# A 212-for-235 transfer rate in a planner, ten wide idle products for nineteen narrow ones, and new due-time offsets, in a Fourier filter followed by a gated convolution

## The chip, the cores and the metric

The kernel runs on one core of one Trainium2 chip. The metric is the device time of one execution in microseconds; the time before is the median of three runs. Lower is better.

## The reference

The input `x` has 8 batches of 3200 positions with 256 channels, in float32. Each batch is transformed along the positions, mixed across channels as complex numbers, soft-thresholded at 0.01 and transformed back; the result goes through a causal five-tap convolution that makes a gate, a product with `w_val` that the gate multiplies, and a product with `w_out`.

```python
X = np.fft.rfft(x, axis=1);  Xr, Xi = X.real, X.imag
Yr = Xr @ w_r - Xi @ w_i + b_r
Yi = Xr @ w_i + Xi @ w_r + b_i
Yr, Yi = (np.sign(v) * np.maximum(np.abs(v) - 0.01, 0) for v in (Yr, Yi))
y = np.fft.irfft(Yr + 1j * Yi, n=3200, axis=1)
gate = sigmoid(sum(conv_w[k] * shifted(y, k) for k in range(5)))
out = (gate * (y @ w_val)) @ w_out
```

## The kernel before, in words

**The transform is split as 3200 = 50 x 64.** Every batch goes through these stages; the names are those of the profile.

1. `p` (L583; L549 for the first batch): the 50-point part. `x` tiles of 50 rows come in by L577 (L540), each tile as two transfers of 200 KB that use ten of the sixteen DMA engines. Four products of 64 output rows with 512 columns fill one PSUM tile; ScalarE copies it out and it goes to a DRAM buffer `a_dram` (L597, L561).
2. `s` (L634): `a` is read back from DRAM (L615) with the other index on the partitions, and a full-float32 product with the constants `f_sb` gives the spectrum with channels on the partitions. There are 13 steps `u` a batch, all but the last with two frequency groups each, so two halves of two products.
3. ScalarE and VectorE split the spectrum into a rounded high part and the rest (`xs`), and make the sum of real and imaginary parts (`sx`) (L684 to L696).
4. The complex mixing by three real products: `k_bank` (L709, six products of 128 x 256) and `y_ps` (L704, twelve). The last step of a batch has a special form (L667, L668). VectorE adds `k_bank` and the bias (L715), then `y_ps` (L718); ScalarE and VectorE threshold (L722, L724) into `tp`.
5. `z_ps` (L747, sixteen products of 64 x 64 weights for two steps; L739 for the last step alone): the inverse 64-point part. ScalarE copies it out (L758, L755), and it goes to `z_dram` (L765).
6. `y_p` (L803): the inverse 50-point part for a block of 400 positions, read back from `z_dram` by L788 (again 200 KB on ten engines). ScalarE copies it into `y_sb` (L810).
7. For each of 8 blocks a batch: VectorE's taps `acc` (L860, four for each half of the channels), ScalarE's first tap and sigmoid (L857, L871), the split of `y` (L360, L362), `v_ps` (L835, twelve products), VectorE's multiplication by the gate (L902), the split into `gated`, `o_ps` (L835), the copy to `o` (L926) and the store to `out` (L928). The last blocks of the last batches use unsplit float32 weights `w_late` (L831).

**TensorE works in three manners.** Products on pieces of 64 x 64 of the array (`p`, `z_ps`, `y_p`), which the code marks "q"; full-float32 products (`s`, L469, L739 and the `w_late` products); and rounded products of 128 x 128 (`k_bank`, `y_ps`, `v_ps`, `o_ps`), marked "r".

**A planner in the program sets the order.** `Plan.add` takes pieces with an engine, a duration, tiles read and written, and a due time `at`. `Plan.order` walks forward in its own model of time: on each engine it considers the pieces that can begin within a small slack of the earliest, and takes the one with the smallest due time; on TensorE it adds or subtracts offsets (`stay`, `crowd`, `hold`, `together`) that make it stay with or away from "q" products. The due times are step numbers plus offsets from the table `O`; one step is a thirteenth of a batch. `PIPE` tells the planner what all transfers of so many engines together move in bytes per ns. None of these numbers is in an instruction: they only set the order in which instructions stand on each engine's queue (TensorE, VectorE, ScalarE, and SyncE for nearly all DMAs), and each queue is then worked off in order.

**PSUM and buffers.** `ps_2` has two tiles of two banks that `p`, `z_ps`, `y_p`, `v_ps` and `o_ps` take in turn, so each of these groups waits until the one two places earlier has been read out. `y_ps` has one tile, `k_bank` two halves. `a` has two tiles of four frequency groups.

**Idle products.** In the first batch TensorE has nothing to do while `x` comes in and `a_dram` makes its way to DRAM and back. `warm` (L947 to L951) issues float32 products on zeros into a PSUM tile that nobody reads: 4 first, one after each `p`, and `WARM[2]` after the eighth `p` (L960, L961). L469 turns `f_sb` blocks into the inverse constants with an identity matrix; its constants come by L456.

## Time and profile before

| | |
|---|---|
| median of three runs | 883.22 us (881.55 to 883.49) |
| the profiled execution | 881.59 us, of which its span is 879.8 us |
| mean granted TensorE clock | 0.994 of full speed |
| VectorE, ScalarE busy | 759.1 us (86%), 604.9 us (69%) |
| DMA | 163.34 MB, 186 GB/s over the span |

The span runs from the first to the last instruction. A timeline row has the start and the length in us, the engine, the line, the operation, output and input, the shapes, and the number of instructions; in brackets stands how long the engine was idle before it and what ended that. One float32 product is two instructions there, so four products `p` are x8 and two steps' `z_ps` x32. Rows of one engine overlap by the pipeline; what a group takes is the distance from its start to the next group's start. In a table of stretches the columns are the stretch, its length, each engine's busy time, the granted clock, the DMA share and GB/s.

### The profile page before, as it was taken

How to read it: one execution, taken by the hardware profiler on the slowest of the kernel's cores; microseconds unless marked ns; L12 is line 12 of the kernel's file. 1: busy time of each engine (PE TensorE's matmuls, PEld its weight loads, DVE VectorE, ACT ScalarE, POOL GpSimd, SP SyncE). 2: the span in 40 equal slices, each digit the busy share in tenths (PEclk: the TensorE clock that was granted, in tenths of full speed). 3: DMA queues.
4: the chain of work that ended last, by engine and by line, in shares of the span. 5: the costliest groups of instructions: out<-in, count | busy, mean ns of one | idle time of the engine just before them, and what ended most of it. 6: DMA issues, size and time to landing. Idle time of an engine off the chain costs nothing.

```text
span 879.8 us, 24544 instructions
## 1 busy us (share of the span) xinstructions
PE 857.8 (97%) x10400; PEld 745.5 (85%) x10400; DVE 759.1 (86%) x1143; ACT 604.9 (69%) x928; POOL 3.8 (0%) x11
## 2 busy tenths in 40 slices
PE   7999999999999999999999999999999999998997
PEld 3778788878999898898899889898899999998775
DVE  2346888999989996999879997899969999899796
ACT  2456666977677766877667776877658775875664
POOL 0000000000000000000000000000100000000000
PEclk9999999999999999999999999999999999999999
DMA  6878886786554476565855576646746353423522
GB/s 212 253 244 253 240 269 197 265 251 199 165 184 146 148 218 212 177 185 172 272 168 171 175 237 205 218 122 208 244 133 202 104 171 94 142 103 110 186 76 94
DMA packets 105289, 163.34 MB, mean 186 GB/s; under 512 B 9690, under 2 KB 78172, under 8 KB 105180
## 3 DMA queue, kind: packets, MB, share of 16 engines
q1 hardware_dynamic: 103764, 158.43, 58.1%
q10 hardware_dynamic: 1416, 3.34, 1.2%
q8 instruction: 82, 1.34, 0.6%
q14 instruction: 27, 0.22, 0.1%
HBM read 82.05 MB, written 79.69 MB: 184 GB/s over the span
## 4 chain that ended last, share of the span: by engine, by line
PE 78%; DVE 15%; DMA 3%; ACT 2%; issue 1%; SPq 0%; ACTq 0%; DVEq 0%
PE y_ps L704 14%; PE o_ps L835 12%; PE v_ps L835 11%; PE s L634 9%; PE z_ps L747 8%; PE k_bank L709 7%; PE y_p L803 6%; DVE acc L860 6%; PE p L583 5%; DMA x<-in_x 2%; PE warm L951 1%; DVE acc L902 1%; PE v_ps L831 1%; DMA f_sb<-in_f 1%; DVE gated L362 1%
## 5 line engine op out<-in xcount | busy, mean ns | idle before, releaser
L860 DVE SCALAR_TENSOR_TENSOR acc<-y_sb,cw_sb,acc 128x800 f32<-128x800 f32 (+1 forms) x264 | 258.7, 1017 | 11.4 <-ACT acc L857 11.2
L704 PE MATMUL y_ps<-w_sb,xs 128*128 128x256 f32 x1152 | 157.7, 286 | 0.7 <-DVE yb L718 0.7
L835 PE MATMUL o_ps<-gated,wo_sb 128*128 128x400 f32 x756 | 153.5, 352 | 0.0
L704 PEld LDWEIGHTS y_ps<-w_sb,xs 128*128 128x128 f32 x1152 | 144.3, 190 | 8.6 <-issue 3.9
L835 PEld LDWEIGHTS o_ps<-gated,wo_sb 128*128 128x128 f32 x756 | 135.6, 189 | 3.4 <-issue 1.0
L835 PE MATMUL v_ps<-y_hl,wv_sb 128*128 128x400 f32 x660 | 130.6, 346 | 1.1 <-ACT y_sb L810 1.1
L634 PEld LDWEIGHTS s<-f_sb,a 128*128 128x128 f32 x800 | 100.3, 191 | 24.9 <-issue 19.0
L835 PEld LDWEIGHTS v_ps<-y_hl,wv_sb 128*128 128x128 f32 x660 | 118.7, 188 | 2.1 <-ACT y_sb L810 1.3
L634 PE MATMUL s<-f_sb,a 128*128 128x128 f32 x800 | 111.9, 280 | 1.3 <-DVE xs L692 1.2
L747 PE MATMUL z_ps<-tp,g_sb 64*64 64x256 f32 x1536 | 93.7, 380 | 0.0
L688 ACT CAST xs<-s 128x512 fp32r<-128x512 f32 x96 | 56.2, 586 | 43.0 <-PE y_ps L704 28.1
L709 PE MATMUL k_bank<-w_sb,xs 128*128 128x256 f32 x576 | 85.3, 283 | 0.4 <-DVE yb L715 0.4
L722 ACT ACTIVATE tp<-yb,nlam 128x512 f32<-128x512 f32 (+1 forms) x104 | 73.6, 708 | 16.5 <-DVE yb L718 9.0
L718 DVE TENSOR_TENSOR yb<-y_ps,yb 128x512 f32<-128x512 f32 x96 | 65.4, 681 | 19.9 <-PE y_ps L704 19.7
L747 PEld LDWEIGHTS z_ps<-tp,g_sb 64*64 64x64 f32 x1536 | 57.1, 133 | 27.1 <-issue 5.8
L360 ACT CAST gated<-acc 128x800 fp32r<-128x800 f32 x63 | 54.2, 861 | 37.1 <-DVE acc L902 33.5
L709 PEld LDWEIGHTS k_bank<-w_sb,xs 128*128 128x128 f32 x576 | 74.8, 188 | 5.1 <-issue 1.1
L926 ACT COPY o<-o_ps 128x800 f32<-128x800 f32 x63 | 51.9, 823 | 38.0 <-PE o_ps L835 37.8
L803 PEld LDWEIGHTS y_p<-g_sb,zl 50*64 50x64 f32 x4096 | 66.1, 135 | 13.9 <-issue 5.1
L902 DVE TENSOR_TENSOR acc<-v_ps,acc 128x800 f32<-128x800 f32 x64 | 62.9, 983 | 16.9 <-PE v_ps L835 14.1
L724 DVE SCALAR_TENSOR_TENSOR tp<-yb,tp 128x512 f32<-128x512 f32 (+1 forms) x104 | 68.8, 661 | 7.7 <-ACT tp L722 7.4
L803 PE MATMUL y_p<-g_sb,zl 50*64 50x50 f32 x4096 | 71.8, 220 | 3.4 <-issue 2.2
(80 smaller groups left out, 1028.4 us busy)
## 6 DMA issues: line engine op xcount, KB each, us to landing
zl<-z_dram SPq DMA_DIRECT2D x128, 200.0 KB
out<-o SPq DMA_DIRECT2D x63, 400.0 KB
a_dram<-s SPq DMA_DIRECT2D x120, 208.0 KB
a<-a_dram SPq DMA_DIRECT2D x96, 256.0 KB
z_dram<-z_t SPq DMA_DIRECT2D x48, 512.0 KB
x<-in_x SPq DMA_DIRECT2D x120, 200.0 KB
a_dram<-s ACTq DMA_DIRECT2D x8, 208.0 KB
x<-in_x ACTq DMA_DIRECT2D x8, 200.0 KB
```

The source lines that it names most:

```text
L634: nc.tensor.matmul(spec()[:, c, :, i, :], tl[ka][:, i0 + i, c * P:(c + 1) * P], f2_of(i), start=True, stop=True)
L688: nc.scalar.copy(out=tl[kx][:, 0:512], in_=tl[k2].rearrange("p a b -> p (a b)"))
L704: nc.tensor.matmul(p[:, 1 - r, :], xm(hx, c, r), w_sb[:, m, hw, c, :], start=k == 0, stop=k == 5)
L709: nc.tensor.matmul(p, sm(hx, c), w_sb[:, 0, hw, c, :], start=k == 0, stop=k == 5)
L718: add(at + 0.2, "DVE", dve(2 * D), lambda: nc.vector.tensor_tensor(out=yb(), in0=tl[ky], in1=yb(), op=ALU.add), [ky + (0,)], [kb + (0,)])
L722: nc.scalar.activation(out=buffer(kt, "tp", [P, 2, D])[:, 0:n], in_=tl[kb][:, 0:n], func=AF.Relu, bias=nlam)
L724: add(at + 0.2, "DVE", dve(n * D), lambda: nc.vector.scalar_tensor_tensor(out=tl[kt][:, 0:n], in0=tl[kb][:, 0:n], scalar=LAM, in1=tl[kt][: ...
L747: nc.tensor.matmul(p[e * HP:(e + 1) * HP, i, j * D:(j + 1) * D], g[i * HP:(i + 1) * HP, r, e * HP:(e + 1) * HP], tl[kts[j]][i * HP:(i + 1) ...
L803: nc.tensor.matmul(pv[h][e * HP:(e + 1) * HP, c, m, :], zt[half(h), m, c * P + e * HP:c * P + (e + 1) * HP], g2_sb[half(h), :], start=True ...
L835: nc.tensor.matmul(p[:, e, 0:TB], w[:, hw, c, e * P:(e + 1) * P], src(hy, c), start=n == 0, stop=n == 5)
L860: nc.vector.scalar_tensor_tensor(out=acc(c), in0=y_of(c, j), scalar=cw_sb[:, c, j:j + 1], in1=acc(c), op0=ALU.mult, op1=ALU.add)
L902: add(at + own("gate", b), "DVE", dve(2 * TB), lambda: nc.vector.tensor_tensor(out=gate(), in0=hn(tl[kv][:, :, 0:TB]), in1=gate(), op=ALU. ...
```

## The change

Three numbers of the planner and the idle products change; no stage, tile or buffer does. The planner is told that transfers on ten engines (`x` and `zl`) move 212 instead of 235 bytes per ns together. Nineteen idle products of 256 columns after the eighth `p` become ten of 512 columns, planned at 860 ns each. Of the offsets in `O`, 33 of 35 have new values (two lines shown). The transfers themselves are as before.

```diff
-PIPE = {10: 235, 13: 300, 16: 324}
+PIPE = {10: 212, 13: 300, 16: 324}
...
-O = {'stay': -42.085,
-     'crowd': -50.453,
+O = {'stay': -8.386,
+     'crowd': 0.988,
...
-WARM = 4, 1, 19
+WARM = 4, 1, 10
...
-    def warm(n):
+    def warm(n, w=2 * P):
...
-            nc.tensor.matmul(pw.rearrange("p a b -> p (a b)")[:, 0:2 * P], tl[ki][:, 0:P], tl[ki][:, 0:2 * P], start=True, stop=True)
+            nc.tensor.matmul(pw.rearrange("p a b -> p (a b)")[:, 0:w], tl[ki][:, 0:P], tl[ki][:, 0:w], start=True, stop=True)
...
-        add(-22, "PE", 430, lambda: warm(1), [ki + (0,), ("turn", "p1", 7)], [kw + ("end", i)], ins=4)
+        add(-22, "PE", 860, lambda: warm(1, 4 * P), [ki + (0,), ("turn", "p1", 7)], [kw + ("end", i)], ins=4)
```

**TensorE's queue in the first batch.** Before, from the first `k_bank` of the mixing on (`s2` is the tile of the profile's `s`, `p1` that of its `p`; the number behind a name tells tiles of one kind apart):

```order
L709 MATMUL k_bank_79<-w_sb_72,xs_293 128x256 x6
L583 MATMUL p1_321<-x_254,f1_sb_68 64x512 x4
L634 MATMUL s2_308<-f2_sb_69,a_247 128x2x64 x2
L583 MATMUL p1_336<-x_261,f1_sb_68 64x512 x4
L704 MATMUL y_ps_347<-w_sb_72,xs_293 128x256 x12
L583 MATMUL p1_365<-x_277,f1_sb_68 64x512 x4
L709 MATMUL k_bank_79<-w_sb_72,xs_305 128x256 x6
L634 MATMUL s2_389<-f2_sb_69,a_247 128x2x64 x2
L469 MATMUL k_bank_79<-eye_sb_66,f2_sb_69 128x128 x2
L634 MATMUL s2_389<-f2_sb_69,a_247 128x2x64 x2
L469 MATMUL k_bank_79<-eye_sb_66,f2_sb_69 128x128 x4
L704 MATMUL y_ps_409<-w_sb_72,xs_305 128x256 x12
```

After, the same place:

```order
L709 MATMUL k_bank_79<-w_sb_72,xs_284 128x256 x6
L583 MATMUL p1_312<-x_245,f1_sb_68 64x512 x4
L704 MATMUL y_ps_320<-w_sb_72,xs_284 128x256 x12
L583 MATMUL p1_341<-x_252,f1_sb_68 64x512 x4
L583 MATMUL p1_349<-x_268,f1_sb_68 64x512 x4
L634 MATMUL s2_299<-f2_sb_69,a_239 128x2x64 x2
L709 MATMUL k_bank_79<-w_sb_72,xs_296 128x256 x6
L704 MATMUL y_ps_372<-w_sb_72,xs_296 128x256 x12
L469 MATMUL k_bank_79<-eye_sb_66,f2_sb_69 128x128 x4
L634 MATMUL s2_401<-f2_sb_69,a_239 128x2x64 x2
L469 MATMUL k_bank_79<-eye_sb_66,f2_sb_69 128x128 x4
L583 MATMUL p1_415<-x_335,f1_sb_68 64x512 x4
```

The second step's `y_ps` now stands ahead of L469, the half `s` that stood ahead of it stands behind four of them, and the fourth `p` of the next batch comes directly after L469.

**TensorE's queue where the last batch's spectrum ends.** Before, from the special form of the last `y_ps` on (one of its twelve rows):

```order
L668 MATMUL y_ps_10314<-w_sb_72,xz_10272 128x256
L835 MATMUL o_ps_10331<-gated_10248,wo_sb_74 128x400 x12
L835 MATMUL v_ps_10352<-y_hl_10190,wv_sb_73 128x400 x12
L747 MATMUL z_ps_10374<-tp_10253,g1_sb_71 64x256 x8
L747 MATMUL z_ps_10374<-tp_10293,g1_sb_71 64x256 x8
L739 MATMUL z_ps_10405<-tp_10349,g1_sb_71 128x256
L835 MATMUL o_ps_10407<-gated_10338,wo_sb_74 128x400 x12
L835 MATMUL v_ps_10426<-y_hl_10327,wv_sb_73 128x400 x12
L835 MATMUL o_ps_10450<-gated_10403,wo_sb_74 128x400 x12
L835 MATMUL v_ps_10470<-y_hl_10391,wv_sb_73 128x400 x12
L831 MATMUL v_ps_10490<-y_sb_78,w_late_8659 128x400 x4
```

After:

```order
L668 MATMUL y_ps_10246<-w_sb_72,xz_10183 128x256
L835 MATMUL v_ps_10264<-y_hl_9947,wv_sb_73 128x400 x12
L835 MATMUL o_ps_10286<-gated_10105,wo_sb_74 128x400 x12
L835 MATMUL v_ps_10306<-y_hl_10094,wv_sb_73 128x400 x12
L835 MATMUL o_ps_10325<-gated_10303,wo_sb_74 128x400 x12
L747 MATMUL z_ps_10344<-tp_10115,g1_sb_71 64x256 x8
L747 MATMUL z_ps_10344<-tp_10244,g1_sb_71 64x256 x8
L835 MATMUL v_ps_10367<-y_hl_10294,wv_sb_73 128x400 x12
L739 MATMUL z_ps_10388<-tp_10282,g1_sb_71 128x256
L835 MATMUL o_ps_10399<-gated_10342,wo_sb_74 128x400 x12
L835 MATMUL v_ps_10419<-y_hl_10332,wv_sb_73 128x400 x12
```

Between the last `y_ps` and L739 stand five groups of L835 where there were two. From `o_ps` behind L739 on, the rows to the end are of the same kinds in the same sequence in both.

**VectorE's queue at the same place.** Before, from the bias of the last `y_ps` on:

```order
L670 TENSOR_TENSOR yb_10340<-y_ps_10314,bias_sb_75 128x256
L362 TENSOR_TENSOR gated_10338<-acc_9963,gated_10338 128x800
L724 SCALAR_TENSOR_TENSOR tp_10349<-yb_10340,tp_10349 128x256
L860 SCALAR_TENSOR_TENSOR acc_10226<-y_sb_78,cw_sb_76,acc_10226 128x800 x4
L362 TENSOR_TENSOR y_hl_10327<-y_sb_78,y_hl_10327 128x800
L362 TENSOR_TENSOR y_hl_10391<-y_sb_78,y_hl_10391 128x800
L902 TENSOR_TENSOR acc_10226<-v_ps_10352,acc_10226 128x4x200
```

After:

```order
L670 TENSOR_TENSOR yb_10272<-y_ps_10246,bias_sb_75 128x256
L860 SCALAR_TENSOR_TENSOR acc_10206<-y_sb_78,cw_sb_76,acc_10206 128x800 x2
L902 TENSOR_TENSOR acc_9861<-v_ps_10264,acc_9861 128x4x200
L724 SCALAR_TENSOR_TENSOR tp_10282<-yb_10272,tp_10282 128x256
L362 TENSOR_TENSOR y_hl_10294<-y_sb_78,y_hl_10294 128x800
L362 TENSOR_TENSOR gated_10303<-acc_9861,gated_10303 128x800
L860 SCALAR_TENSOR_TENSOR acc_10206<-y_sb_78,cw_sb_76,acc_10206 128x800 x2
L902 TENSOR_TENSOR acc_9861<-v_ps_10306,acc_9861 128x4x200
L860 SCALAR_TENSOR_TENSOR acc_10206<-y_sb_78,cw_sb_76,acc_10206 128x800 x2
L362 TENSOR_TENSOR gated_10342<-acc_9861,gated_10342 128x800
L860 SCALAR_TENSOR_TENSOR acc_10206<-y_sb_78,cw_sb_76,acc_10206 128x800
L362 TENSOR_TENSOR y_hl_10332<-y_sb_78,y_hl_10332 128x800
```

After these rows stand one tap, the L902 that reads `v_ps_10367`, and then one more `y_hl`. Before, four taps and two splits stood between the threshold (L724) and the L902 that frees a `ps_2` tile; now the L902s stand two taps apart.

**Turns between manners over the whole queue.** Counting neighbours in TensorE's rows, the 64 x 64 products are entered 90 times before and 81 times after (from rounded products 64 and 55, from float32 products 26 and 26) and left 90 and 81 times (to float32 51 and 34, to rounded 39 and 47). A rounded product follows a float32 one 100 times before and 113 times after; the other way it is 75 and 105. `k_bank` stands directly behind `s` 5 times before and 75 times after, `y_ps` 52 times and 4 times.

More of the change, by code (lines that the diff above doesn't have):

```diff
@@ L256 @@
 T = float(NU)
-O = {'stay': -42.085,
-     'crowd': -50.453,
-     'hold': 7.335,
-     'together': 155.775,
-     'later': 18.484,
-     'load_x': 192.178,
-     'p1': -1.787,
-     'p1_step': 1.293,
-     'load_a': -41.005,
-     's2': -2.447,
-     's1i': 2.145,
-     'p3': 2.825,
-     'load_z': -29.254,
-     'y': 3.704,
-     'conv': 5.188,
-     'val': 5.514,
-     'gate': -19.992,
-     'project': 8.565,
+O = {'stay': -8.386,
+     'crowd': 0.988,
+     'hold': -136.589,
+     'together': 54.115,
+     'later': 35.92,
+     'load_x': 206.961,
+     'p1': -6.98,
+     'p1_step': 1.767,
+     'load_a': -59.069,
+     's2': -1.728,
+     's1i': 2.55,
+     'p3': 1.483,
+     'load_z': -110.046,
+     'y': 5.286,
+     'conv': 6.343,
+     'val': 4.902,
+     'gate': -104.312,
+     'project': 7.158,
      'late_val': 7.079,
      'late_out': 15.503,
-     'turn': -153.706,
-     'mix_sum': -0.971,
-     'p1_1': -89.715,
-     'load_x_1': 85.875,
-     'p1_2': 25.498,
-     'p3_6': -1.759,
-     'p3_7': -0.606,
-     'y_7': 18.885,
-     'conv_7': -29.176,
-     'val_7': 13.441,
-     'gate_7': -17.01,
-     'project_7': 13.598,
-     'p3_1': -0.93,
-     'p1_3': -6.723,
-     'p3_0': 0.056}
-WARM = 4, 1, 19
+     'turn': -116.746,
+     'mix_sum': -0.545,
+     'p1_1': -62.001,
+     'load_x_1': 103.471,
+     'p1_2': 52.478,
+     'p3_6': 1.616,
+     'p3_7': 2.132,
+     'y_7': -5.19,
+     'conv_7': -129.677,
+     'val_7': 24.144,
+     'gate_7': -93.128,
+     'project_7': 24.183,
+     'p3_1': 2.362,
+     'p1_3': -3.214,
+     'p3_0': 4.249}
+WARM = 4, 1, 10
 SLOTS = {"x": 3, "zl": 3, "y_hl": 2, "s1": 3, "a": 2, "xs": 2, "sx": 2, "xz": 1, "yb": 2, "tp": 3, "zst": 2,
```

## The prediction

> **What bounds the kernel now.** I read the page's head first, then the stretches, the waits of TensorE, the chain that ended last, and the timeline where the stretches show TensorE idle.
>
> ```profile
> span 879.8 us, 24544 instructions
> PE 857.8 (97%) x10400; PEld 745.5 (85%) x10400; DVE 759.1 (86%) x1143; ACT 604.9 (69%) x928; POOL 3.8 (0%) x11
> ```
>
> ```profile
> 32.00:48.00 16.00, 14.27 (x94) 9.84 (x93) 8.70 (x16) 9.32 (x19) 0.00 (x0) 1.00 0.90 219
> 48.00:52.00 4.00, 2.30 (x18) 1.92 (x17) 1.75 (x4) 1.39 (x3) 0.00 (x0) 1.00 0.70 241
> 52.00:56.00 4.00, 3.73 (x20) 3.73 (x21) 0.42 (x1) 1.14 (x4) 0.00 (x0) 0.61 0.87 311
> 56.00:110.00 54.00, 53.64 (x527) 41.87 (x526) 39.70 (x81) 35.30 (x62) 0.00 (x0) 1.00 0.83 244
> 110.00:750.00 640.00, 636.85 (x8024) 570.40 (x8022) 588.43 (x890) 466.49 (x718) 2.69 (x2) 1.00 0.62 190
> 804.00:807.00 3.00, 2.83 (x8) 2.68 (x9) 3.00 (x5) 1.23 (x2) 0.00 (x0) 0.50 0.61 213
> ```
>
> The span is TensorE's: it is idle 22.0 us in all and only 3.5 us between 56 and 750. So the change can win in two ways: TensorE's own work gets shorter (only turns between manners and idle products can), or its gaps do. There are two dear gaps, around 50 us and around 803 us, and each is followed by a stretch at a lower granted clock (0.61 and 0.50).
>
> The profiled execution took 881.59 us, 1.63 below the median and at the low end of its three runs. I make the sum against it and carry the difference over to 883.22.
>
> **Part 1, ten wide idle products.** The chain that ended last, early on:
>
> ```profile
> 24.28 6.20 PE warm L951 x20
> 30.92 3.89 PE warm L951 x18
> 36.98 2.04 PE s L634 x16
> 40.32 9.99 DMA f_sb<-in_f
> ```
>
> The idle products are on the path: the first `s` starts behind them without waiting for its data. The second nine took 3.89 us, 0.43 each. Ten of 512 columns are as many columns as twenty of 256, so the first five take as long as the ten did and the second five one old product more: +0.43 us. The `f_sb` load of 9.99 us is issued behind an `a` load that waits for this `s`, so it moves by as much. The cover, if that wait hid it, would make it 0; I take 0.4.
>
> **Part 2, turns between manners.** What a group takes, by who stands next to it:
>
> ```profile
> 310.87 0.59 PE L739 MATMUL z_ps<-tp,g_sb 128*128 128x256 f32 x2
> 311.30 1.05 PE L634 MATMUL s<-f_sb,a 128*128 128x128 f32 x8
> ...
> 318.68 1.05 PE L634 MATMUL s<-f_sb,a 128*128 128x128 f32 x8
> 319.49 1.65 PE L704 MATMUL y_ps<-w_sb,xs 128*128 128x256 f32 x12
> 320.98 0.86 PE L709 MATMUL k_bank<-w_sb,xs 128*128 128x256 f32 x6
> 321.77 1.96 PE L747 MATMUL z_ps<-tp,g_sb 64*64 64x256 f32 x32
> 323.54 1.04 PE L583 MATMUL p<-x,f_sb 50*64 50x512 f32 x8
> 324.51 1.16 PE L634 MATMUL s<-f_sb,a 128*128 128x128 f32 x8
> 325.43 2.41 PE L835 MATMUL o_ps<-gated,wo_sb 128*128 128x400 f32 x12
> 327.68 1.57 PE L704 MATMUL y_ps<-w_sb,xs 128*128 128x256 f32 x12
> 329.09 0.86 PE L709 MATMUL k_bank<-w_sb,xs 128*128 128x256 f32 x6
> 329.79 2.35 PE L835 MATMUL v_ps<-y_hl,wv_sb 128*128 128x400 f32 x12
> 331.98 1.05 PE L634 MATMUL s<-f_sb,a 128*128 128x128 f32 x8
> 332.96 1.09 PE L583 MATMUL p<-x,f_sb 50*64 50x512 f32 x8
> 333.87 1.91 PE L747 MATMUL z_ps<-tp,g_sb 64*64 64x256 f32 x32
> 335.60 1.04 PE L583 MATMUL p<-x,f_sb 50*64 50x512 f32 x8
> ```
>
> `y_ps` takes 1.41 behind a rounded product (327.68) and 1.49 behind float32 (319.49): a rounded product behind a float32 one costs 0.08, and a float32 one behind a rounded one nothing (`s` 0.81 at 318.68). `k_bank` takes 0.70 (329.09) and 0.79 ahead of `z_ps` (320.98); `z_ps` 1.77 on entry and 1.73 in the middle of its manner; so rounded to 64 x 64 is 0.13. `s` takes 0.98 ahead of `p` (331.98) against 0.81: with the 0.04, 0.21 from float32. Leaving costs `p` 0.97 against 0.91 with its own entry in it (0.04), so 0.10, and the next group about as much again (`s` 0.92 against 0.81): 0.21.
>
> By the counts given with the change: before 64 x 0.13 + 26 x 0.21 + 90 x 0.21 + 100 x 0.08 = 40.7 us; after 55 x 0.13 + 26 x 0.21 + 81 x 0.21 + 113 x 0.08 = 38.7. That is -2.0 us, nine entries and exits fewer against thirteen float32-to-rounded turns more. It is TensorE's own time on the path, and I give it 0.5 either way.
>
> **Part 3, the gap around 50 us.**
>
> ```profile
> 40.16 0.68 PE L634 MATMUL s<-f_sb,a 128*128 128x128 f32 x4 [1.16 <-DVE xs L692]
> ...
> 48.53 0.61 PE L634 MATMUL s<-f_sb,a 128*128 128x128 f32 x4
> 50.36 0.71 PE L469 MATMUL k_bank<-eye_sb,f_sb 128*128 128x128 f32 x4 [1.22 <-DMA f_sb<-in_f]
> 50.91 0.61 PE L634 MATMUL s<-f_sb,a 128*128 128x128 f32 x4
> 52.27 1.58 PE L469 MATMUL k_bank<-eye_sb,f_sb 128*128 128x128 f32 x8 [0.75 <-ACT g_sb L471]
> 53.50 2.90 PE L704 MATMUL y_ps<-w_sb,xs 128*128 128x256 f32 x12
> 56.21 0.64 PE L469 MATMUL k_bank<-eye_sb,f_sb 128*128 128x128 f32 x4
> ```
>
> L469 waits 1.22 for `f_sb`, then 0.75 for ScalarE to free a half of `k_bank`, and the `y_ps` behind takes 2.71 (53.50 to 56.21) instead of 1.5 at the lower clock: 3.2 us lost. Afterwards a whole `y_ps` (1.5) stands ahead of this L469 and a half `s` (0.4) less, so TensorE arrives 1.1 us later by its own work, while part 1 moves it and `f_sb` alike: the wait shrinks to about 0.1. I leave 0.7 in all, for what of the work ahead of it was itself waiting for `x`. ScalarE's two copies are covered, since four turning products and a half `s` stand between where two did. With under 1.2 idle in one piece the clock should hold: the 1.16 at 40.16 lies in a stretch of 1.00. So 2.5 us can go. Against it: the fourth and fifth `p` come some 3 us earlier, their `x` loads stand behind `f_sb` in the one queue, and the DMA share is 0.83 from 56 to 110. Any wait there eats the gain. Bounds: +1.0 (`x` late by 3, clock kept) and -3.2; I take -2.0, nearer the timeline's gap than the load I cannot see.
>
> **Part 4, the gap around 803 us.** TensorE, then VectorE:
>
> ```profile
> 804.17 1.19 PE L739 MATMUL z_ps<-tp,g_sb 128*128 128x256 f32 x2 [2.93 <-DVE acc L902]
> 804.80 3.63 PE L835 MATMUL o_ps<-gated,wo_sb 128*128 128x400 f32 x12
> ```
>
> ```profile
> 797.39 3.93 DVE L860 SCALAR_TENSOR_TENSOR acc<-y_sb,cw_sb,acc 128x800 f32<-128x800 f32 x4
> 801.24 1.88 DVE L362 TENSOR_TENSOR y_hl<-y_sb,y_hl 128x800 fp32r<-128x800 f32 x2
> 803.05 0.98 DVE L902 TENSOR_TENSOR acc<-v_ps,acc 128x800 f32<-128x800 f32 x1
> ```
>
> L739 waits 2.93 for a PSUM tile, because VectorE does four taps and two splits before the L902 that frees it. Then the clock is at 0.50: L739 takes 0.63 against 0.43 (310.87), the next `o_ps` 3.63 against 2.41 (325.43). Lost: 2.93 + 0.2 + 1.2 = 4.3 us.
>
> Afterwards, counting from the end of the last `y_ps`: the tile for the `o_ps` behind L739 is freed by the third L902 in VectorE's rows. Up to and with it stand eight taps at 0.96 (3.85 from the four's start to the split), three L902 and four splits at 0.9 (1.81 for two), and two operations on a third of the columns, some 0.35 each: 14.7, and with a lag of 0.3 at the start, which is my choice, 15.0. TensorE's rows up to there are five groups of 2.19 (329.79 to 331.98), `z_ps` at 1.8, a turn back at 0.2 and L739 at 0.43: 13.4. So it waits some 1.6 instead of 2.93, in one piece shorter than what lowered the clock and not far above the 1.16 that did not. Gain 2.7. Bounds: 1.0, if VectorE comes a microsecond later still and the clock falls again, and 3.5, if the wait is under a microsecond. What is late next is VectorE again; behind L739 both queues are of the same kinds to the end, and I give that end no change.
>
> [...]
>
> **Part 5, everything between.** From 110 to 750 TensorE is idle 3.2 us. The new order has all new neighbours, `k_bank` now close behind `s` where `y_ps` was. Below, all of that idle time could go (-3); above, I allow twice as much again (+6). No row shows the new neighbours; I take +1.0, nearer to the idle time of before. The 212 for 235 changes no transfer: it only plans `x` and `zl` later, and costs nothing but through the order.
>
> **The sum.** 881.59 + 0.4 - 2.0 - 2.0 - 2.7 + 1.0 = 876.3, that is -5.3. On the median: 883.22 - 5.3 = 877.9.
>
> **The rivals.**
>
> 1. *The gaps only move.* Parts 3 and 4 give nothing (the `x` loads take the place of `f_sb`, VectorE is as late somewhere else), parts 1, 2 and 5 stay: -0.6, 882.6. For it: VectorE's three rows before 804 follow each other without a break, and the DMA share is 0.83 or more up to 110. Against: the two places have concrete rows moved in the right direction. Chance 0.18.
> 2. *The clock falls by the moment.* If the clock falls after such gaps in some executions only, the 1.4 at 804 and the 1.2 at 53 are not there to be won in the others, and -5.3 becomes -2.7: 880.5. [...] For it: the runs before spread by 1.9 us. Against: the profiled run, which has both, is among the fastest. Chance 0.12.
> 3. *The loads of the first two batches become the bound* (slower). Up to 180 us `x` and `a` are read through one queue, at a DMA share of 0.90 and 0.83 in the stretches above; if the new order asks for them before they land, TensorE stands as it did for `f_sb`, 1.22, and pays 1.2 at the lower clock, 2.4 a time. Parts 1, 2, 4 and 5 sum to -3.3, part 3 is gone; from two such waits on nothing is won, four give -3.3 + 9.6 = +6.3: 889.5. Against: after 56 us no wait on a DMA is among TensorE's idle time. Chance 0.12.
>
> **Chances.** Mine 0.58. 0.2% is 1.77 us, about what a measurement of this kernel can tell from no change: faster means below 881.45, slower above 884.99. Mine gives 0.55 faster and 0.03 same; the second rival 0.08 and 0.04; the first 0.05, 0.12 and 0.01; the third 0.12 slower: 0.68, 0.19, 0.13. The range goes from 873.5 (both gaps at their better ends and part 5 at -1) to 883.5, which takes in the second rival and most of the first. My case's own range is 874 to 881.
>
> **What would show it.** After the change: the idle products take 8.5 us of columns and the first `s` starts 0.4 later; `y_ps` near 50 us takes about 1.5 with the clock at 1.00; L739 starts without a long wait and the `o_ps` behind it waits 1 to 2 for L902; TensorE's idle time is 1 to 3 us smaller and its busy time about 4 (2 in turns, 2.6 at the lower clock, less 0.4). I am wrong if TensorE shows waits on `x` or `a` before 180 us, more than 5 us idle between 110 and 750, or a stretch near the end at 0.50.

## The result, and the profile after

| | before | after |
|---|---|---|
| median of the runs | 882.38 us (4 runs) | 891.58 us (4 runs) |
| ratio, 95% interval | 1 | 1.0130 (1.0106 to 1.0154) |
| profiled execution | 881.59 us | 891.34 us |
| TensorE idle in the span | 22.0 us | 29.4 us |
| of which with the releaser "issue" | 2.2 us | 9.6 us |

The change is slower by 1.3%. The page of the changed kernel begins:

```profile
span 889.1 us, 24479 instructions
PE 859.7 (97%) x10382; PEld 742.0 (83%) x10382; DVE 760.3 (86%) x1143; ACT 603.7 (68%) x928; POOL 5.6 (1%) x11
```

TensorE is idle 7.4 us longer and busy 1.9 us longer; 0.4 of the 9.75 lies outside the span. The same stretches as in the prediction:

```profile
48.00:52.00 4.00, 3.70 (x32) 3.51 (x31) 2.85 (x6) 2.22 (x6) 0.00 (x0) 1.00 0.75 252
52.00:56.00 4.00, 4.00 (x51) 2.00 (x49) 0.40 (x1) 2.58 (x4) 0.00 (x0) 1.00 0.74 247
56.00:110.00 54.00, 52.82 (x522) 42.88 (x520) 39.89 (x83) 34.19 (x64) 0.00 (x0) 1.00 0.88 259
110.00:750.00 640.00, 626.28 (x7855) 559.84 (x7848) 579.62 (x870) 458.17 (x702) 4.46 (x2) 0.99 0.61 186
```

The gap around 50 us is nearly closed, and the clock stays at 1.00 where it was 0.61. But between 110 and 750 TensorE is idle 13.7 us; it was 3.15. The gap around 803 us is gone too, in the timeline of TensorE:

```profile
812.03 0.59 PE L739 MATMUL z_ps<-tp,g_sb 128*128 128x256 f32 x2
813.47 2.44 PE L835 MATMUL o_ps<-gated,wo_sb 128*128 128x400 f32 x12 [0.84 <-ACT z_t L755]
```

So both gaps that the prediction went for were won, and more was lost elsewhere. The waits of TensorE say with what; the first row is of the kernel before, the three below it are of the changed one (the columns are the total in us, how often, and the longest):

```profile
PE y_p L803 <- issue: 2.2, 5, 1.0
```

```profile
PE y_p L803 <- issue: 5.8, 6, 1.6
PE y_ps L704 <- issue: 3.1, 1, 3.1
...
PE s L634 <- issue: 0.7, 1, 0.7
```

"Issue" means that TensorE waited for nothing that the profile shows: no other engine, no semaphore, no load of data. It is 9.6 us where it was 2.2, and these 7.4 us are the whole growth of the idle time. All other idle time of TensorE sums to 19.8 us in both kernels: what the two gaps gave back was taken by small waits elsewhere. The "issue" rows in the timeline of the changed kernel, with the rows around the two longest:

```profile
278.84 0.49 PE L634 MATMUL s<-f_sb,a 128*128 128x128 f32 x2 [0.68 <-issue]
...
297.27 1.08 PE L803 MATMUL y_p<-g_sb,zl 50*64 50x50 f32 x58
299.99 0.33 PE L803 MATMUL y_p<-g_sb,zl 50*64 50x50 f32 x6 [1.63 <-issue]
300.25 1.52 PE L634 MATMUL s<-f_sb,a 128*128 128x128 f32 x8
301.42 1.63 PE L709 MATMUL k_bank<-w_sb,xs 128*128 128x256 f32 x6
...
449.64 0.49 PE L803 MATMUL y_p<-g_sb,zl 50*64 50x50 f32 x17 [0.24 <-issue]
489.90 0.32 PE L803 MATMUL y_p<-g_sb,zl 50*64 50x50 f32 x5 [0.94 <-issue]
552.51 0.74 PE L803 MATMUL y_p<-g_sb,zl 50*64 50x50 f32 x36 [0.46 <-issue]
566.15 0.20 PE L803 MATMUL y_p<-g_sb,zl 50*64 50x50 f32 x1 [1.21 <-issue]
...
663.48 1.10 PE L803 MATMUL y_p<-g_sb,zl 50*64 50x50 f32 x64
664.51 0.97 PE L704 MATMUL y_ps<-w_sb,xs 128*128 128x256 f32 x6
668.53 0.86 PE L704 MATMUL y_ps<-w_sb,xs 128*128 128x256 f32 x6 [3.06 <-issue]
669.24 1.64 PE L634 MATMUL s<-f_sb,a 128*128 128x128 f32 x8
670.53 3.52 PE L835 MATMUL v_ps<-y_hl,wv_sb 128*128 128x400 f32 x12
...
831.07 0.45 PE L803 MATMUL y_p<-g_sb,zl 50*64 50x50 f32 x16 [1.36 <-issue]
```

The stalls fall into the middle of groups: 58 products of a `y_p` run, then TensorE stands, then the last 6. The 64 are one piece with one set of operands, and what the 58 had, the 6 had too. Behind the two longest the granted clock is 0.50 (from 300.9 to 304.3 and from 669.5 to 672.9): eight `s` take 1.52 and 1.64, six `k_bank` 1.63, a `v_ps` 3.52.

**Theory A: TensorE ran out of instructions.** The list of DMA queues on the changed kernel's page has a queue that carries no data:

```profile
q8 instruction: 82, 1.34, 0.6%
```

82 packets of 1.34 MB in all are 16 KB each. The trace records 10382 matmuls and as many weight loads, 20764 in all, so a packet holds some 253 of them, or 256 if about 1% of what it holds has no record. Counted between the stalls, there are these many matmuls (the number in brackets behind the second figure):

```profile
278.84:299.99 21.15, 19.52 (x255) 18.75 (x255) 19.97 (x29) 15.17 (x24) 0.00 (x0) 1.00 0.58 200
...
489.90:552.51 62.61, 62.16 (x634) 56.67 (x634) 55.57 (x85) 43.37 (x67) 0.00 (x0) 1.00 0.58 173
...
668.53:831.07 162.54, 158.83 (x2032) 147.65 (x2032) 154.01 (x220) 110.36 (x167) 0.00 (x0) 0.99 0.41 128
```

With as many weight loads these are 510, 1268 and 4064 instructions: 2, 5 and 16 times 256 to within 1%. The landings fit as well: in the trace each of the eight stalls ends 1.3 to 1.6 us after a packet of this queue has landed (299.99 after one at 298.64, 668.53 after one at 667.02). So TensorE stands at the borders of its 256-instruction blocks, at those where the next block has come too late. A slide of a border to another product changes whether a dense run of short products (`y_p`: 64 matmuls and as many weight loads in 1.03 us, from 663.48 to 664.51) outruns the next block. The new order moved every one of them.

The kernel itself has these blocks, which the description above leaves out. The planner counts each piece's TensorE instructions (`ins`), and L241 gives it blocks of 256 (`PACKET`) and constants for when a block is asked for and how long it takes to come (`TRIGGER`, `FETCH`, `QUEUE`), which no run here measures; L165 to L167 hold a piece back until its block is there. Followed to its end, this model has TensorE wait 1.8 us for blocks in the kernel before and not at all in the changed one, and the changed one end 5.6 us sooner (858.6 for 864.2). The chip shows 2.2 and 9.6 us. So the new order was planned with the blocks in view, and TensorE outran them all the same.

**Theory B:** the new order itself makes TensorE wait for VectorE, ScalarE or a transfer, and the halved clocks follow. **Theory C** came up with the first runs: the shape of the idle products, or the moment at which step 1 begins, makes the difference.

The edit 212 for 235 needed no run. With that number alone changed, in either kernel, the order of the rows is the same on every engine.

### The profile page after: what moved, and what is told of

Its sections match the earlier page's. It is cut to its first block, busy times and chain, and to the rows that moved or that the text cites. A ratio compares the mean times of both kernels' runs of the same rounds, so it can differ in the third digit from the quotient of the medians.

```text
span 889.1 us, 24479 instructions
## 1 busy us (share of the span) xinstructions
PE 859.7 (97%) x10382; PEld 742.0 (83%) x10382; DVE 760.3 (86%) x1143; ACT 603.7 (68%) x928; POOL 5.6 (1%) x11
## 3 DMA queue, kind: packets, MB, share of 16 engines
q8 instruction: 82, 1.34, 0.6%
## 4 chain that ended last, share of the span: by engine, by line
PE 69%; DVE 20%; DMA 4%; ACT 3%; issue 3%; ACTq 0%; DVEq 0%; SPq 0%
PE y_ps L704 12%; PE o_ps L835 11%; PE v_ps L835 10%; PE s L634 8%; DVE acc L860 8%; PE z_ps L747 7%; PE k_bank L709 6%; PE y_p L803 5%; PE p L583 5%; DMA zl<-z_dram 2%; DVE acc L902 2%; DVE gated L362 2%; DVE tp L724 1%; PE warm L951 1%; DVE yb L715 1%
## 5 line engine op out<-in xcount | busy, mean ns | idle before, releaser
L860 DVE SCALAR_TENSOR_TENSOR acc<-y_sb,cw_sb,acc 128x800 f32<-128x800 f32 (+1 forms) x264 | 262.9, 1021 | 10.5 <-ACT acc L857 10.0
L835 PE MATMUL o_ps<-gated,wo_sb 128*128 128x400 f32 x756 | 150.6, 348 | 0.8 <-ACT z_t L755 0.8
L835 PEld LDWEIGHTS o_ps<-gated,wo_sb 128*128 128x128 f32 x756 | 135.3, 188 | 3.8 <-ACT z_t L755 1.2
L835 PE MATMUL v_ps<-y_hl,wv_sb 128*128 128x400 f32 x660 | 131.6, 348 | 0.7 <-DVE acc L902 0.7
L835 PEld LDWEIGHTS v_ps<-y_hl,wv_sb 128*128 128x128 f32 x660 | 118.2, 190 | 2.7 <-issue 1.2
L634 PEld LDWEIGHTS s<-f_sb,a 128*128 128x128 f32 x800 | 102.5, 192 | 16.1 <-issue 12.6
L709 PE MATMUL k_bank<-w_sb,xs 128*128 128x256 f32 x576 | 91.5, 294 | 1.7 <-ACT xs L688 1.7
L803 PE MATMUL y_p<-g_sb,zl 50*64 50x50 f32 x4096 | 74.1, 220 | 9.5 <-issue 5.8
L715 DVE TENSOR_TENSOR yb<-k_bank,bias_sb 128x512 f32<-128x512 f32 x96 | 65.4, 681 | 13.6 <-PE k_bank L709 13.6
L724 DVE SCALAR_TENSOR_TENSOR tp<-yb,tp 128x512 f32<-128x512 f32 (+1 forms) x104 | 68.8, 662 | 8.7 <-ACT tp L722 8.7
L902 DVE TENSOR_TENSOR acc<-v_ps,acc 128x800 f32<-128x800 f32 x64 | 62.9, 983 | 8.6 <-PE v_ps L835 5.6
L871 ACT ACTIVATE acc<-acc 128x800 f32<-128x800 f32 (+1 forms) x66 | 55.7, 854 | 16.9 <-DVE acc L860 16.1
```

Source lines behind the costliest of these rows:

```text
L634: nc.tensor.matmul(spec()[:, c, :, i, :], tl[ka][:, i0 + i, c * P:(c + 1) * P], f2_of(i), start=True, stop=True)
L709: nc.tensor.matmul(p, sm(hx, c), w_sb[:, 0, hw, c, :], start=k == 0, stop=k == 5)
L715: nc.vector.tensor_tensor(out=buffer(kb, "yb", [P, 2, D]), in0=tl[kk].rearrange("p (a d) -> p a d", a=1).to_broadcast([P, 2, D]), in1=bias ...
L724: add(at + 0.2, "DVE", dve(n * D), lambda: nc.vector.scalar_tensor_tensor(out=tl[kt][:, 0:n], in0=tl[kb][:, 0:n], scalar=LAM, in1=tl[kt][: ...
L803: nc.tensor.matmul(pv[h][e * HP:(e + 1) * HP, c, m, :], zt[half(h), m, c * P + e * HP:c * P + (e + 1) * HP], g2_sb[half(h), :], start=True ...
L835: nc.tensor.matmul(p[:, e, 0:TB], w[:, hw, c, e * P:(e + 1) * P], src(hy, c), start=n == 0, stop=n == 5)
```

## The experiments

**Sliding the borders.** Splitting an idle product into narrower ones adds TensorE instructions ahead of all else, with the same columns in sum and no other row moved. An added product is four instructions (two weight loads, two matmuls: with thirty products more, a_split4's page has 10442 of each for 10382). The edit is to line 961; the four kernels have

```
-    lambda: warm(1, 4 * P)
+    lambda i=i: warm(2, 2 * P) if i < 4 else warm(1, 4 * P)      # a_split4of10, 16 more
+    lambda: warm(2, 2 * P)                                       # a_split2, 40 more
+    lambda: (warm(2, 171), warm(1, 170))                         # a_split3, 80 more
+    lambda: warm(4, P)                                           # a_split4, 120 more
```

The stalls expected of each were worked out from the changed kernel's trace: the points in the list at which a block must have landed were moved by that number of instructions, and the time of each block from its point of asking to its landing was kept; where that point lies was the author's estimate, which no run shows.

> The changed kernel, with four of its ten wide idle products before the turn of step 1 written as two products of 256 columns each: 16 TensorE instructions more (a product of 32-bit numbers is 2 weight loads and 2 matmuls), the same columns, and every other row of every engine in the same order. Theory A (TensorE ran out of fetched instructions: its stream comes in blocks of 16 KB, 256 instructions each, and it stands when a block lands late; where the block borders fall in the order sets how often): by sliding the places of the borders along the changed kernel's own trace, against the landings of its blocks, 16 instructions leave them in the same dense runs, 9 to 11 us of stalls as before: 889 to 893 us. Theory B (the new order makes TensorE wait for VectorE, ScalarE or a transfer): nothing that it rests on is moved: 890 to 893 us. So both say no change; it is the control for the three kernels beside it.

> The changed kernel, with each of the ten wide idle products written as two of 256 columns: 40 TensorE instructions more, the same columns, no other row moved. Theory A: sliding the borders of the instruction blocks by 40 along the changed kernel's trace leaves 5 to 9 us of stalls of some 10: 885 to 890 us. Theory B: 890 to 893 us, as the changed kernel.

> The changed kernel, with each of the ten wide idle products written as three, of 171, 171 and 170 columns: 80 TensorE instructions more, the same columns, no other row moved. Theory A: sliding the borders by 80 leaves about 2 us of stalls of some 10, and with the stalls the halved clocks behind the longer ones go: 880 to 884 us, and the trace shows under 4 us of TensorE's idle time with the releaser 'issue' (9.6 in the changed kernel). Theory B: 890 to 893 us, and those rows stay or are other engines' rows.

> The changed kernel, with each of the ten wide idle products written as four of 128 columns: 120 TensorE instructions more, the same columns, no other row moved. Theory A: sliding the borders by 120 leaves about 2 us of stalls: 880 to 885 us. Theory B: 890 to 893 us.

Measured, with the changed kernel at the top ("issue" is the sum of those rows in the one profiled execution; the last column is the span less the start of the first `s`, which takes the start out; ratios are to the kernel before):

| kernel | instructions more | median us | ratio, 95% interval | "issue" us | first `s` | from there to the end |
|---|---|---|---|---|---|---|
| after | 0 | 891.58 | 1.0130 (1.0106 to 1.0154) | 9.6 | 36.9 | 852.2 |
| a_split4of10 | 16 | 890.38 | 1.0115 (1.0074 to 1.0156) | 6.7 | 36.0 | 855.2 |
| a_split2 | 40 | 887.25 | 1.0096 (1.0066 to 1.0127) | 6.6 | 36.7 | 847.9 |
| a_split3 | 80 | 884.10 | 1.0035 (1.0007 to 1.0062) | 4.8 | 38.5 | 842.7 |
| a_split4 | 120 | 881.70 | 0.9994 (0.9970 to 1.0017) | 0.6 | 37.8 | 838.8 |

The control stays slow (its stalls are 6.7 us, fewer than expected, with a mean clock of 0.986 for 0.994) and the others fall step by step, to no difference from the kernel before. Theory B is out as the cause of the loss, since no row that it rests on was moved. One size was missed: a_split3 kept 4.8 us of stalls where about 2, and under 4, were expected. Two of the ten runs of a_split4 took 1049.52 and 1197.06 us, at mean granted clocks of 0.752 and 0.654; the other eight lie between 877.7 and 883.2, with a median of 880.56. The same place as around 668 us, in the timeline of a_split4:

```profile
656.37 0.38 PE L803 MATMUL y_p<-g_sb,zl 50*64 50x50 f32 x10
657.32 1.03 PE L803 MATMUL y_p<-g_sb,zl 50*64 50x50 f32 x54 [0.57 <-issue]
658.28 1.67 PE L704 MATMUL y_ps<-w_sb,xs 128*128 128x256 f32 x12
659.78 1.05 PE L634 MATMUL s<-f_sb,a 128*128 128x128 f32 x8
660.59 2.42 PE L835 MATMUL v_ps<-y_hl,wv_sb 128*128 128x400 f32 x12
```

It is the same sequence of groups. The border now falls behind ten of the `y_p` and not into the `y_ps`, the stall is 0.57 for 3.06, and the clock holds: `s` 1.05 for 1.64, `v_ps` 2.42 for 3.52. This is its only "issue" row.

**The same slide in the kernel before, and each half of the change alone.** The first kernel splits the nineteen idle products of before; the second has the new offsets with the old idle products and 235; the third has the old offsets with the new idle products.

```
-    lambda: warm(1)
+    lambda: warm(2, P)                           # b_split2, on before

-    add(-22, "PE", 860, lambda: warm(1, 4 * P)   # offsets_only, on after
+    add(-22, "PE", 430, lambda: warm(1)
-WARM = 4, 1, 10
+WARM = 4, 1, 19

-    add(-22, "PE", 430, lambda: warm(1)          # warm_only, on before
+    add(-22, "PE", 860, lambda: warm(1, 4 * P)
-WARM = 4, 1, 19
+WARM = 4, 1, 10
```

> The kernel before, with each of its nineteen idle products of 256 columns ahead of the turn of step 1 written as two of 128 columns: 76 TensorE instructions more, the same columns, no other row moved on any engine. Theory A (the instruction blocks' borders): sliding the borders by 76 along the trace of before takes them out of a lucky place: 4 us of stalls in place of 1.5 to 2.2, and some halved clock behind them if one is long: 1.5 to 5 us slower than before, ratio 1.002 to 1.006. Theory B (stalls belong to the new order alone, and before has no such trouble): ratio 1.000.

> The changed kernel's offsets alone, with the nineteen idle products of 256 columns of before (36 TensorE instructions more than the changed kernel) and 235 bytes per ns. The rows of TensorE differ from the changed kernel's at some 110 lines of its list, so the borders can't be slid exactly. Theory A: by the slide of 36 along the changed kernel's trace some 5 to 9 us of stalls: 885 to 890 us. Theory B (the new offsets make the loss by their waits, wherever the borders fall): 890 to 893 us.

> The offsets of before with ten idle products of 512 columns (36 TensorE instructions fewer than before, and some 200 lines of TensorE's list differ from it). Theory A: sliding the borders by 36 the other way along the trace of before gives 5 to 6 us of stalls in place of 1.5 to 2.2, one of them above 2 us: 883 to 888 us. Theory B: the offsets of before don't lose anything: 880 to 882 us.

b_split2: 883.96 us against 881.33, ratio 1.0019 (1.0003 to 1.0035). The "issue" rows of its waits:

```profile
PE y_p L803 <- issue: 5.2, 6, 1.8
```

That is 3.0 us more than before's 2.2, for no other edit than 76 instructions at the start. Before's borders lie in a good place, as theory A has it; whether by luck or by the planner's count of the blocks is open. The cost in time is at the low end of what was expected.

offsets_only: 886.72 us, ratio 1.0054 (1.0034 to 1.0074), in the range that theory A gave but not by its mechanism: "issue" is 2.3 us, as before. Its span is 4.8 us longer than before's, 2.7 of it idle time at other waits. What these offsets are worth apart from the borders is therefore not settled by this kernel, which has another order than the changed one.

warm_only: 900.62 us, ratio 1.0206 (1.0182 to 1.0229), slower than either theory gave (in the planner's own model too it ends 16.7 us after the kernel before), and with 2.4 us of "issue". The largest row of its waits, and the timeline at the longest of them:

```profile
PE s L634 <- DVE xs L692: 7.2, 3, 4.3
```

```profile
775.50 0.81 PE L634 MATMUL s<-f_sb,a 128*128 128x128 f32 x4 [4.29 <-DVE xs L692]
...
779.85 1.65 PE L709 MATMUL k_bank<-w_sb,xs 128*128 128x256 f32 x6
```

So this half fails in theory B's way: the planned 860 ns pieces lead to another order with the old offsets, in which `s` waits 4.29 for VectorE and a lower clock follows (0.77 in the mean from 775 to 790; six `k_bank` take 1.65 for 0.87). Offsets and idle products belong together, and the halves don't add up to the change.

**Are the blocks late because of the kernel's own transfers?** One kernel takes traffic away, by storing 16 of 128 partitions of the output (the rest of the output is left out); one, on a_split4, adds some.

```
-    nc.sync.dma_start(out=dst, in_=tl[ko])
+    nc.sync.dma_start(out=dst[0:16], in_=tl[ko][0:16])                   # a_out16
+    [nc.sync.dma_start(out=dst, in_=tl[ko]) for _ in range(2)]           # a_split4_out2, a_split4_out2b
```

> The changed kernel, in which 63 of the 65 stores of the output write 16 of their 128 partitions (the rest of the output is left out): 22 MB of the 163 MB that are moved fall away, and TensorE's rows and its instruction blocks stand as in the changed kernel. Theory A1 (a block lands late because it queues behind the kernel's own transfers): the stalls with the releaser 'issue' shrink from 9.6 to 4 to 7 us, and the time to 883 to 888 us. Theory A2 (a block's way is long whatever else moves, and only the dense runs of short instructions outrun it): the stalls stay at 8 to 11 us and the time at 889 to 893 us.

a_out16: 891.00 us, ratio 1.0094 (1.0068 to 1.0119). The stalls stay, 8.9 us:

```profile
PE y_p L803 <- issue: 4.4, 8, 1.4
PE y_ps L704 <- issue: 3.2, 1, 3.2
PE s L634 <- issue: 1.3, 1, 1.3
```

22 MB less of 163 don't bring the blocks in time. This speaks for theory A2.

> The kernel with each wide idle product as four of 128 columns, in which 63 of the 65 stores of the output are issued twice: 25 MB more beside 163 MB, TensorE's rows and block borders as without. Theory A1 (blocks land later when the kernel's own transfers are heavier): stalls with the releaser 'issue' come back, 3 to 7 us in place of 0.6, and 884 to 890 us. Theory A2 (a block's way does not depend on that much load): under 2 us of them, 880 to 884 us.

a_split4_out2: 921.38 us, ratio 1.0453 (1.0409 to 1.0497), far beyond both. Its profiled execution took 2944 us and shows another thing (below), so it was taken again:

> The kernel with the doubled output stores once more, for a profile. It took 915 to 925 us in four of its five runs, far past what either theory gave (884 to 890 or 880 to 884). Theory A1 (late instruction blocks): most of the 35 us stands as 'issue' ahead of TensorE's rows. Theory D (the doubled stores hold SP's queue and the transfers behind them): most of it stands as waits for zl, x or a, or for the engines behind those, and 'issue' stays under 5 us.

a_split4_out2b: 914.88 us, ratio 1.0382 (1.0341 to 1.0422). The rows of its waits:

```profile
PE y_p L803 <- DMA zl<-z_dram: 17.2, 17, 4.3
...
PE y_p L803 <- issue: 1.0, 1, 1.0
```

Theory D holds: the doubled stores delay `zl`, and "issue" stays at 1.0. With 14% of the traffic away or 15% more, the stalls stay about what the borders make them. That the load has no part in a block's delay is not shown by this: a seventh less did not bring the blocks in time, and with a seventh more TensorE's 17.2 us of waiting for `zl` can also have given them more time to land.

**Borders or narrow products (theory C)?** If the borders are what counts, 256 instructions more must bring the loss back.

```
-    lambda: warm(1, 4 * P)                       # a_plus256
+    lambda i=i: warm(8, 64) if i < 5 else (warm(6, 64), warm(1, P)) if i < 6 else warm(4, P)
-    lambda: warm(WARM[0])
+    lambda: warm(2 * WARM[0], P)
-    lambda: warm(WARM[1])
+    lambda: warm(2 * WARM[1], P)

-    lambda: warm(1, 4 * P)                       # a_narrower
+    lambda: warm(4, 116)
```

> The changed kernel, with its 21 idle products written as 85 narrower ones of 64 and 128 columns, the same columns in sum: 256 TensorE instructions more, one whole instruction block, and no other row moved. Theory A (where the borders of blocks of 256 instructions fall): every border falls where it does in the changed kernel, so the stalls come back: 8 to 13 us of 'issue', 889 to 894 us. Theory C (narrow idle products help of themselves, by the clock or by the moment at which step 1 begins): as with four products in place of one, 880 to 884 us.

> The changed kernel, with each of the ten wide idle products written as four of 116 columns: 120 TensorE instructions more, and 9% fewer idle columns; no other row moved. In the kernel with four of 128 columns the idle work ended about 1 us after the changed kernel's and that much later than the f_sb load asked for. Theory A: the stalls stay away, and the start gains 0.5 to 1 us: 880 to 882 us, ratio 0.997 to 1.000 of before.

a_plus256: 903.37 us, ratio 1.0254 (1.0215 to 1.0292), later than both. The granted clock was 0.51 from 27 to 43 us, under the products of 64 columns, and the first `s` started at 54.8, 17.9 us later than in the changed kernel. From there to the end it took 851.5 us, against 852.2 there and 838.8 in a_split4, with 9.2 us of "issue". That is theory A's number, but with so different a start it was no clean test.

a_narrower: 883.62 us, ratio 1.0033 (1.0008 to 1.0057). The start gained 0.9 us (first `s` at 36.8), and "issue" is 0.5; but the time did not fall below a_split4's. The expected gain did not come, and no version here beats the kernel before. Its profiled execution had a mean granted clock of 0.992, a_split4's of 0.995; six `k_bank` at 49.58 took 1.42 us to the next group, where those at 40.46 took 0.88.

The clean test puts the instructions where TensorE waits for `x`, as small products in the 64 x 64 manner of the `p` behind them:

```
+    def small(n):
+        pw = tl[kw]
+        for _ in range(n):
+            nc.tensor.matmul(pw.rearrange("p a b -> p (a b)")[0:HP, 0:N2], tl[ki][half(0), 0:HP], tl[ki][half(0), 0:N2], start=True, stop=True)
...
-    lambda: warm(WARM[1])
+    lambda u=u: (warm(WARM[1]), small(5 if u < 6 else 4))       # a_small34; with warm(4, P) as well: a_small34_split4
```

> The changed kernel, with 34 small products (64 by 50 by 50, in a corner of the array) put behind the seven idle products between the pieces of step 1: 136 TensorE instructions more in a stretch in which TensorE waits for x; the ten wide idle products stay as they are, and no other row is moved. Theory A (borders of the blocks of 256): sliding the borders by 136 leaves 2 to 3 us of stalls: 881 to 885 us. Theory C (narrower idle products before the turn of step 1 were what helped): these are as wide as in the changed kernel, so 890 to 893 us.

> Both edits that each add about half a block: the 34 small products (136 instructions) and each wide idle product as four of 128 columns (120 instructions), 256 in all. Theory A: the borders fall again where they fall in the changed kernel, and the stalls come back, 8 to 12 us of 'issue': 889 to 893 us, although each edit alone gives 881 to 885. Theory C: the narrow idle products help here as they did alone: 880 to 884 us.

| | ten products of 512 columns | forty of 128 (+120) |
|---|---|---|
| without the small products | 891.58 us, "issue" 9.6 | 881.70 us, "issue" 0.6 |
| with 34 small products (+136) | 884.55 us, "issue" 2.6 | 890.83 us, "issue" 6.8 |

The ratios are 1.0040 (1.0007 to 1.0073) for a_small34 and 1.0109 (1.0062 to 1.0156) for both edits. The runs of a_small34 spread from 879.6 to 888.0 us, with one at 893.6, so its own size is loose; one of the four of both edits took 903.84, and the other three have a median of 888.34. Not all of their time is the blocks': the first `s` starts at 38.6 us in a_small34 and at 40.7 with both edits. From there to the end they take 838.9 and 845.5 us, against 838.8 in a_split4 and 852.2 in the changed kernel. So each edit alone takes the loss away behind the first `s`, and both together bring half of it back, with 6.8 of the 9.6 us of stalls. Theory C falls; of the theories here only a count that comes round at 256 does this. The timeline of a_small34_split4 shows the stalls at the same products as in the changed kernel:

```profile
301.77 0.33 PE L803 MATMUL y_p<-g_sb,zl 50*64 50x50 f32 x6 [1.36 <-issue]
...
450.12 0.49 PE L803 MATMUL y_p<-g_sb,zl 50*64 50x50 f32 x17 [0.50 <-issue]
490.92 0.32 PE L803 MATMUL y_p<-g_sb,zl 50*64 50x50 f32 x5 [1.16 <-issue]
553.77 0.74 PE L803 MATMUL y_p<-g_sb,zl 50*64 50x50 f32 x36 [0.65 <-issue]
567.47 0.20 PE L803 MATMUL y_p<-g_sb,zl 50*64 50x50 f32 x1 [1.26 <-issue]
667.31 0.86 PE L704 MATMUL y_ps<-w_sb,xs 128*128 128x256 f32 x6 [0.50 <-issue]
828.02 0.45 PE L803 MATMUL y_p<-g_sb,zl 50*64 50x50 f32 x16 [1.06 <-issue]
```

The last 6 of a run, the last 17, 5, 36, 1, 6 and 16: the same counts, row for row, and each stands 256 recorded instructions later in TensorE's queue (the page has 10510 matmuls and as many weight loads, for 10382). One stall of the changed kernel, at 278.84, has no counterpart, behind a wait for `zl` that grew from 0.36 to 0.92, and one of 0.31 at 846.89 is new. The lengths differ too, 0.50 for 3.06 at the `y_ps`: the places of the stalls went with the order, and their lengths differed between the two executions.

## Why the prediction was wrong

Forecast were 877.9 us, range 873.5 to 883.5, faster. It became 891.6, slower.

- **The step that failed is part 5**, "No row shows the new neighbours; I take +1.0, nearer to the idle time of before", with bounds of -3 and +6. From 110 to 750 TensorE is idle 10.6 us more (13.7 for 3.15): 7.5 are "issue" and 3.1 waits for other engines and for `zl`. The bounds were multiples of before's idle time and asked for no cause; the second kind stays inside them, and the first, late instruction blocks, was put at nothing. A row of before showed it: `y_p` with 2.2 us of "issue" in five stalls, the second largest sum among TensorE's waits. The prediction does not mention it, nor the planner's lines on the blocks. Had either been followed to the 16 KB packets, the forecast would have had a term that a new order draws afresh: in the runs here 0.5 to 9.6 us of idle time, with before's 2.2 near the good end.
- To the stalls comes the clock behind them. At 300 us eight `s` and six `k_bank` took 1.52 and 1.63 where they take 1.05 and 0.87 at full clock, 1.2 us; at 669 `s` and `v_ps` took 1.64 and 3.52 for 1.05 and 2.42, 1.7 us: some 3 us in all. So 7.4 and 3 are 10.4 us, and the rest of the sum -0.7.
- **Part 1** (+0.4): the first `s` starts at 36.93, where it was 36.98. The second five idle products took 4.46 where the second nine took 4.05, so the 0.4 is there, but they all began 0.2 sooner and nothing of it reached the `s`.
- **Part 2** (-2.0) did not show. In a_split4, almost without stalls, TensorE's busy time less that of the idle products is 858.5 - 20.3 = 838.2 us; before it is 857.8 - 18.2 = 839.6. In these -1.4 the two halved clocks of before, 1.2 and 1.4 by parts 3 and 4, are -2.6, and a halved clock of a_split4 itself, behind 140, is some +1.6 (from `s` at 140.13 to the end of `y_ps` 4.8 us, where the changed kernel takes 3.2). That leaves some -0.4 for the turns. The `k_bank` groups took 6.1 us more (91.4 for 85.3), so the turns were moved rather than saved. A price from one stretch, for turns by a count of neighbours, was too bold; which turns cost more was not tried.
- **Part 3** (-2.0) was right, in part by luck. In the stretches from 32 to 56 the idle time falls from 3.7 to 1.9 us and the clock stays at 1.00, some -3.0 in all, of which the clock's 1.2 hangs on the moment (see the second rival); from 56 to 110 the idle time grows by 0.8, of which 0.70 is a wait of `k_bank` for ScalarE's `xs`, not for `x` as the reason against it had it.
- **Part 4** (-2.7) was right in kind and better in size. L739 starts without a wait, `o_ps` waits 0.84 and not 1.6, for ScalarE's `z_t` and not for L902, and the clock holds: 2.1 of idle and 1.4 of clock, at its better bound of 3.5. Behind it, where no change was given, some 1.1 us of other waits came in (0.73 for L902 at 820.98).
- **The rivals.** The first had half of it: the two gaps closed, but their idle time came back in small waits, 19.8 us outside "issue" in both kernels. The second was right about the gap around 50 us and about waits of that length, as the rows below show; after the 2.93 at 803 the clock fell in b_split2 as in before (the `o_ps` behind L739 took 3.65 and 3.63). The third had the sign, and nearly the number (889.5), by a mechanism that is not there: TensorE waits neither for `a` nor longer for `x` than before (for `zl` it waits 1.5 us in all), and from 32 to 110 it is idle 3.1 us where it was 4.1. That "more than 5 us idle between 110 and 750" would prove the forecast wrong was the useful sentence: it did.
- **What was right in sum:** with the borders slid to a good place, the changed kernel has a profiled time of 878.74 us, 2.85 under before's 881.59, and behind the first `s` 838.8 us for 842.8. These are single executions: its median of 881.70 us doesn't differ from before (0.9994, 0.9970 to 1.0017). Even without the stalls, most of the forecast gain of 5.3 us is not there.

The rows on the second rival: b_split2 has the rows of before, and around 50 us nearly the same waits (0.75 is the second), but `y_ps` took 1.65 where it took 2.90.

```profile
50.18 0.71 PE L469 MATMUL k_bank<-eye_sb,f_sb 128*128 128x128 f32 x4 [1.11 <-DMA f_sb<-in_f]
...
53.00 1.65 PE L704 MATMUL y_ps<-w_sb,xs 128*128 128x256 f32 x12
```

The changed kernel and a_split4 share the wait ahead of this `p`, and only in a_split4, the second pair of rows, the clock fell behind it:

```profile
137.35 1.09 PE L583 MATMUL p<-x,f_sb 50*64 50x512 f32 x8 [1.64 <-ACT y_sb L810]
138.37 1.16 PE L634 MATMUL s<-f_sb,a 128*128 128x128 f32 x8
```

```profile
139.11 1.09 PE L583 MATMUL p<-x,f_sb 50*64 50x512 f32 x8 [1.63 <-ACT y_sb L810]
140.13 1.53 PE L634 MATMUL s<-f_sb,a 128*128 128x128 f32 x8
```

## What to carry to other kernels

Idle time of TensorE whose releaser is "issue", in the middle of a group of short products, was a late block of instructions here, and the landings on the instruction queue tell. When a change reorders or adds TensorE instructions, every block border behind it falls elsewhere, so part of the difference between two orders is luck, even where a planner counts the blocks; before judging an order, run it with a few dozen idle instructions more at the start, in a place where TensorE waits anyway. Here 120 or 136 such instructions were worth 7 to 10 us of 891, and with both, 256 in all, most of the stalls were back.

## What the runs showed of the hardware

- TensorE's instructions came during the run, in 82 packets of 16 KB for 256 instructions each, and in the changed kernel runs of some 128 instructions per us outran them: single stalls up to 3.06 us, 9.6 us in all of 889. It went on 1.3 to 1.6 us after the packet had landed.
- In the changed kernel the granted clock fell to 0.50 after 1.63 us of idle time (299.99) as after 3.06 (668.53), both times for 3.41 us, and held at 1.00 after 1.36 (831.07): the 24 `o_ps` behind that took 4.61, and 4.64 in a_split4. The length alone does not decide: after 1.64 at 137.35 the clock held at 1.00, and after the same wait of 1.63 in a_split4 the rows behind it took what they take at 0.50 (`k_bank` 1.63 for 0.95, as at 301.42). What decides was not shown.
- In one execution of a_split4_out2, of 2944 us, TensorE was busy 2935.6 us where a_split4 has 858.5, about a third of its speed; VectorE's and ScalarE's busy times, 787.5 and 621.3, were within some 4% of a_split4's 759.9 and 602.5. The clock of 1.00 that is listed for it says nothing, since its page has no row of the clock. One of its rows, with the busy time in us and the mean ns of one:

```profile
L835 PE MATMUL o_ps<-gated,wo_sb 128*128 128x400 f32 x756 | 511.6, 936 | 0.5 <-ACT z_t L755 0.5
```

  The changed kernel's `o_ps` takes 348 ns.
- Half as many columns saved nothing at the halved clock: the matmuls of idle products of 64 columns followed each other by 0.21 us in a_plus256 at a granted clock of 0.51 (80 of them from 26.75 to 43.30). Those of 128 columns followed by 0.11 in a_split4 at 1.00 (40 of them from 31.22 to 35.69), which would be 0.22 at half the clock, an estimate from these rows.
